# Row-tiled scores for two more head pairs, a token mixer by two pairs, and loads ordered by due time, in a block-sparse attention with a ResMLP behind it

## The chip, the cores and the metric

One core of one Trainium2 chip runs the whole program. The metric is the device time of one execution in microseconds (us). The kernel before takes 315.21 us, the median of five runs (314.22 to 315.86).

The engines are named as in the profile: PE is TensorE's matmul, PEld its weight load, DVE is VectorE, ACT is ScalarE, POOL is GpSimd and SP is SyncE. ACT, POOL and SP also issue transfers. L859 means line 859 of the kernel before.

## What is computed

Block-sparse attention over 4 batches, 8 heads, 768 positions and a head dimension of 64, and behind it a ResMLP block with a token mixer and a channel mixer. The reference, cut:

```python
scores = scale * np.matmul(q, k.transpose(0, 1, 3, 2))      # scale 1/8
mask = ...            # blocks of 32: neighbours, first and last, 3 sampled ones for each block of queries
attn = softmax(np.where(mask, scores, -1e9))
x = np.matmul(attn, v)                   # heads side by side: (4, 768, 512)
a1 = alpha1 * x + beta1
tok = np.einsum('ts,bsd->btd', w_tok, a1)                   # w_tok 768 x 768
u = x + lam * tok
a2 = alpha2 * u + beta2
out = u + lam * (np.maximum(a2 @ w_ch1, 0.0) @ w_ch2)       # w_ch1 512 x 2048, w_ch2 2048 x 512
```

All inputs and the output are 32-bit floats. The same mask serves every batch and head.

## The kernel before

**Pairs and units.** Two heads of a batch make a pair, so there are 16 pairs (`NP`), four for each batch. The scores of a pair, 9216 columns in all, are cut into 9 units of 1024 columns (`UN`), 144 units in all. Each unit goes through the scores' matmuls into a PSUM tile `sps` (there are two), one exponential on ACT (L869) into a buffer `eT` (seven), and the matmuls with the values (L895), whose stationary side is `eT` and whose moving side is `vext` with 65 columns, the last of them ones, so that the row sums come out beside the result. At the end of each head, L911 and L914 divide and write the head's columns of `x_sb`.

**Two forms of scores.** For pairs below `T0` = 6, `prep_full` turns queries and keys by PE transposes through the identity (L402, 12 for a pair) and four copies (L447 on ACT or L449 on DVE). The scores (L840) contract over 88 rows: 64 of the head and 24 that carry the mask as a bias. From pair 6 on, `prep_rows` turns them by DMA transposes that SP issues (L753 twice for the queries, L776 for the keys) into `qk`, and two more transfers from POOL (L796, called swaps below) copy query halves to the other half of the partitions. The scores (L859) then contract over 64 rows in each half of the array, the two halves beside each other, and two units are issued as one batch. The mask is not part of these scores: the exponential is multiplied by a mask tile on DVE (L876, 1024 columns). The mask tile is made once, in `mask_ops`, by 12 matmuls (L645) on the `qk` of pair `T0 - 1` and six exponentials (L666). There are two `qk` tiles, four buffers each for the loaded `q`, `k` and `v`, and three `vext`.

**The mixers.** For each pair L1061 and L1072 make `a1p`, 36 matmuls (L1107) of 128 columns multiply it by the turned token weights `wtokT` in two groups of three tiles, L1131 adds the result to `x_sb` and L1138 scales it into `ub`. `ub` is turned into `uT` by PE transposes and copies in batch 0 and for pair 15, by a DMA transpose from SP (L1203) otherwise. When the four pairs of a batch are there, the channel mixer follows in two halves: 16 times four matmuls of 384 columns (L1234), each four closed by a ReLU on ACT (L1256) or DVE (L1264) into `hts` (two buffers), then 48 matmuls of 512 columns (L1296), and L1318 and L1337 give the output out.

**Order.** The first pair is prepared by hand-written instructions before the plan: loads from SP, ACT and POOL (L352 to L363), keep-warm matmuls on zeros (L369), casts (L397), two small matmuls for the mask's rows (L407), transposes (L402), copies (L421). All the rest is ordered by `Plan`: each operation has a due time in units (about one exponential each), the engines that may run it with modelled durations, the operations that it depends on and the buffers that it needs; at each modelled instant the ready operation that is due first is emitted. `SEEDS` shifts some due times by random amounts. `pin_order` then fixes the order on each engine, so an instruction that waits on the chip holds everything behind it on its engine. The loads from memory all go over POOL's queue in one chain, `chain`, in the order of the text: pair 1, the token weights, pair 2, three vectors, pair 3, a vector and a bias, half of `w1b`, pair 4, the other half, pair 5, a quarter of `w2b`, pair 6, the rest of `w2b`, then pairs 7 to 15. Each load is modelled to land after the one before it.

Of the kernel before, what the change touches and what calls it, by code (L numbers as in the profile page):

```python
# [43 lines left out]
T0 = 6  # L44
FINE = 3
SEEDS = [4000001, 4000004, 4000014, 4000025, 4000032, 4000033, 4000038, 4000259, 4000302, 4000315, 4000516, 4000717, 4000744, 4000751, 4000754, 4000772, 4000823, 4000910, 4001214, 4001220, 4002279]
# [52 lines left out]
class Plan:  # L99
# [3 lines left out]
    def __init__(self, pools, free):  # L103
        self.pools = {k: list(range(n)) for k, n in pools.items()}
        self.free = dict(free)
        self.ops = []
        self.users = {}
        self.slot = {}
        self.held = {}
        self.reader = {}  # L110
        self.exps = 0
        self.dma = 0.0
# [47 lines left out]
    def run(self):  # L160
# [13 lines left out]
        while count:  # L174
# [4 lines left out]
            while moved:  # L179
# [35 lines left out]
                if best:  # L215
# [5 lines left out]
                    op.eng = e  # L221
                    if callable(vis):
                        vis = vis(self, t)
                    op.vis = t + vis
                    if op.reads:
                        self.reader[op.reads] = (e, op.vis)
                    self.free[e] = t + occ
# [26 lines left out]
def kernel(  # L254
# [81 lines left out]
    a1p = many(2, [P, NT, P], BF, "a1p")  # L336
    ub = many(2, [P, NT, P], BF, "ub")
# [18 lines left out]
    nc.scalar.dma_start(identb[:], ident_dr.ap())  # L356
    nc.sync.dma_start(kx2[0][MB, 0, :], ind_dr.ap())
    nc.sync.dma_start(q2f[:, 1, :], pair_ap(q, 0, 0)[:, 1, :])
    nc.sync.dma_start(k2f[:, 1, :], pair_ap(k, 0, 0)[:, 1, :])
    for i in range(1, 4):  # L360
        nc.sync.dma_start(kx2[i // 2][MB, i % 2, :], ind_dr.ap())

    nc.gpsimd.dma_start(ld["v"][0][:], pair_ap(v, 0, 0))  # L363
# [58 lines left out]
    keep_warm(5, P)  # L422
    for j in range(1, 4):
        nc.sync.dma_start(qx2[j // 2][MB, j % 2, :], qx2[0][MB, 0, :])

    nc.gpsimd.tensor_copy(out=hold[MB, :], in_=mbb[MB, :])

# [3 lines left out]
        dict(PE=5800, ACT=6100, DVE=5600, POOL=4200, SP=6500),  # L431
# [20 lines left out]
    def dma_vis(cost, issue):  # L452
        def f(plan, t):
            plan.dma = max(plan.dma, t + issue + 1200) + cost
            return plan.dma + 800 - t

        return f

    chain = [None]

    def load(name, cost, due, emit, **kw):
        op = pl.add(
            name, [("POOL", 720, dma_vis(cost, 720))], due, emit, after=chain[-1:], **kw
        )
        chain.append(op)
        return op
# [8 lines left out]
    def load_pair(pi, what="qkv"):  # L475
        b, n = divmod(pi, NPAIR)
        for w in what:
# [6 lines left out]
            LD[key] = load(("load",) + key, 1020, 9 * pi - 20, emit, need=[(key, [(w, 0)])])  # L484
# [6 lines left out]
    def bc_load(nm, t, src):  # L491
# [3 lines left out]
        BC[nm] = load(("bc", nm), 640, 0, emit)  # L495
# [24 lines left out]
    LD[("v", 0)] = landed(("v", 0), 6000)  # L520
    pl.slot[("v", 0)] = ("v", 0)
    pl.pools["v"].remove(0)
    load_pair(1)
    for g in range(3):
        WT.append(load(("wtk", g), 2500, 0, emit_wtk(g)))
    load_pair(2)
    bc_load("lam", lam_bc, moe_lam)
    bc_load("a1", a1_bc, moe_alpha1)
    bc_load("b1", b1_bc, moe_beta1)
    load_pair(3)  # L530
    bc_load("a2", a2_bc, moe_alpha2)
    BE2 = load(("be2",), 300, 0, emit_be2)
    for g in range(2):
        W1.append(load(("w1", g), 2530, 0, emit_w1(g)))
    load_pair(4)
    for g in range(2, 4):
        W1.append(load(("w1", g), 2530, 0, emit_w1(g)))
    load_pair(5)
# [24 lines left out]
    for g in range(4):  # L563
        if g == 1:
            load_pair(6)
        W2.append(
            load(("w2", g), 2530, 0, emit_w2(g), deps=[x.tr for x in WTT])
        )
    for pi in range(7, NP):
        load_pair(pi)  # L570
# [173 lines left out]
    def prep_rows(pi):  # L744
# [3 lines left out]
        def tvis(x):  # L748
            return lambda plan, t: x

        def e_q(op, h):
# [5 lines left out]
            [("SP", 900, tvis(4200))],  # L757
# [8 lines left out]
            [("SP", 900, tvis(4200))],  # L766
# [7 lines left out]
        def e_k(op):  # L774
# [8 lines left out]
            [("SP", 1300, tvis(4200))],  # L783
# [7 lines left out]
        for r in range(2):  # L791

            def e_s(op, r=r):
                i = sl(key)
                lo, hi = slice(r * D, (r + 1) * D), slice((1 - r) * D, (2 - r) * D)
                nc.gpsimd.dma_start(qx2[i][lo, :, HS:S], qx2[i][hi, :, 0:HS])  # L796
# [4 lines left out]
                    [("POOL", 720, tvis(3300))],  # L801
# [9 lines left out]
    for i in range(2):  # L811
# [5 lines left out]
            deps=[landed(("f", i), 5500 + 500 * i)],  # L817
# [571 lines left out]
```

The softmax here doesn't subtract the row's maximum and nothing guards it: scores larger than these inputs give would overflow.

## Time and profile before

| what | value |
|---|---|
| median of five runs | 315.21 us |
| time of the profiled execution | 314.9 us |
| its span, first to last instruction | 313.1 us |
| PE busy | 307.5 us |
| DVE busy | 231.4 us |
| ACT busy | 179.7 us |
| POOL busy | 55.7 us |
| scores by the full form, L840 | 144 matmuls, 33.4 us busy |
| scores by rows, L859 | 240 matmuls, 27.3 us busy |
| token mixer, L1107 | 576 matmuls, 38.2 us busy |
| mask multiplies, L876 | 90, 685 ns each |
| exponentials, L869 | 144, 1022 ns each |
| first exponential | 8.45 us |
| first L1234 of batch 0 | 57.6 us |
| last exponential | ends 244.3 us |
| first L1234 of batch 3 | 259.1 us |

How to read it: busy time of PE is modelled, and matmuls overlap, so the sum over lines is more than the time that they add. What one matmul adds is the distance from its start to the next start. The windows split the span into stretches of 10 us with the busy time of each engine in them; the chain of waits follows the work that ended last back to the start. A DMA share is the mean over 16 DMA engines, and is above 1 where several transfers share an engine.

### The profile page before, as it was taken

To read this page: it belongs to the slowest core of one execution; us is meant where nothing else is said; L and a number is where in the kernel's file an instruction comes from. 1 tells how busy PE (TensorE), PEld (TensorE's weight loads), DVE (VectorE), ACT (ScalarE), POOL (GpSimd) and SP (SyncE) were. 2 spreads that over 40 slices of the span, in tenths; PEclk is the share of its full clock that TensorE was granted. 3 is DMA by queue.
4 is the path that set the end of the run, shared out by engine and by line. 5 is a ranking of instruction groups with operands and counts; after the bars stand their busy time and mean duration, and the time that the engine had idled before them with its cause. 6 is when DMAs were issued, how large, how long until landed. Compare 5 with 4: busy or idle time off the path is not lost.

```text
span 313.1 us, 7718 instructions
## 1 busy us (share of the span) xinstructions
PE 307.5 (98%) x3252; PEld 189.1 (60%) x3252; DVE 231.4 (74%) x434; ACT 179.7 (57%) x215; POOL 55.7 (18%) x87
## 2 busy tenths in 40 slices
PE   7999999999999999999999999999999999999996
PEld 3687888765565656565656565655656555555543
DVE  4569997967797988979878686978878776565631
ACT  4899999895766686867675766557575400000000
POOL 6456443150402140304010100110000000000000
PEclk9999999999999999999999999999999999999999
DMA  8999999999356875378442322332102001100012
GB/s 180 194 236 222 209 204 206 191 118 110 75 91 111 126 115 122 98 113 128 73 110 61 78 60 61 87 75 61 27 33 61 33 2 39 62 36 33 36 51 83
DMA packets 46742, 31.40 MB, mean 100 GB/s; under 512 B 27212, under 2 KB 42292, under 8 KB 46708
## 3 DMA queue, kind: packets, MB, share of 16 engines
q0 software_dynamic: 16944, 17.44, 34.0%
q1 hardware_dynamic: 29440, 13.24, 18.0%
q8 instruction: 25, 0.41, 0.5%
q10 hardware_dynamic: 324, 0.23, 0.3%
q14 instruction: 9, 0.07, 0.1%
HBM read 30.86 MB, written 6.29 MB: 119 GB/s over the span
## 4 chain that ended last, share of the span: by engine, by line
PE 93%; DVE 3%; DMA 1%; ACT 1%; ACTq 0%; issue 0%
PE gb L1234 27%; PE gb L1296 26%; PE gb L895 12%; PE gb L1107 10%; PE sps L859 8%; PE sps L840 7%; PE gb L402 2%; DMA identb<-ident_c 1%; ACT eT L869 1%; PE sps L645 1%; DVE qk L449 1%; PE gb L600 0%; DVE x_sb L1131 0%; DVE ub L1138 0%; DVE a1p L1072 0%
## 5 line engine op out<-in xcount | busy, mean ns | idle before, releaser
L869 ACT ACTIVATE eT<-sps 128x1024 f16<-128x1024 f32 x144 | 139.9, 1022 | 36.7 <-PE sps L859 29.0
L1234 PE MATMUL gb<-uT,w1b 128*128 128x384 bf16 x512 | 100.0, 326 | 0.0
L1296 PE MATMUL gb<-w2b,hts 128*128 128x512 bf16 (+2 forms) x400 | 96.4, 370 | 0.0
L1264 DVE TENSOR_SCALAR hts<-gb,b1t 128x384 bf16<-128x384 f32 x76 | 46.9, 617 | 29.4 <-PE gb L1234 28.9
L1234 PEld LDWEIGHTS <-w1b 128*128 128x128 bf16 x512 | 46.8, 97 | 34.5 <-issue 2.0
L876 DVE TENSOR_TENSOR eT<-eT,msk 128x1024 f16<-128x1024 f16 x90 | 60.4, 685 | 6.1 <-ACT eT L869 6.1
L895 PEld LDWEIGHTS <-eT 128*128 128x128 f16 x1152 | 49.8, 98 | 21.7 <-issue 4.7
L895 PE MATMUL gb<-vext,eT 128*128 128x65 f16 x1152 | 58.1, 194 | 0.1
L1296 PEld LDWEIGHTS <-hts 128*128 128x128 bf16 x400 | 35.7, 97 | 31.2 <-issue 0.7
L1256 ACT ACTIVATE hts<-gb,b1t 128x384 bf16<-128x384 f32 x52 | 30.1, 582 | 28.1 <-PE gb L1234 26.4
L1107 PE MATMUL gb<-a1p,wtokT 128*128 128x128 bf16 x576 | 38.2, 219 | 0.1
L1107 PEld LDWEIGHTS <-wtokT 128*128 128x128 bf16 x576 | 33.9, 98 | 5.6 <-issue 2.6
L840 PE MATMUL sps<-qk 88*128 88x512 bf16 (+1 forms) x144 | 33.4, 340 | 0.3 <-ACT eT L869 0.2
L796 POOL DMA_DIRECT2D qk<-qk x20 | 12.1, 611 | 121.2 <-DMA qk<-q 58.7
L859 PE MATMUL sps<-qk 64*128 64x512 bf16 (+1 forms) x240 | 27.3, 326 | 0.0
L1318 DVE TENSOR_TENSOR ot<-x_sb,gb 128x512 f32<-128x512 f32 (+2 forms) x25 | 16.6, 664 | 10.1 <-PE gb L1296 9.6
L1131 DVE TENSOR_TENSOR x_sb<-x_sb,gb 128x384 f32<-128x384 f32 x32 | 17.7, 552 | 8.0 <-PE gb L1107 7.7
L914 DVE TENSOR_TENSOR x_sb<-gb,rcp 128x384 f32<-128x384 f32 x32 | 17.8, 558 | 1.1
L1138 DVE TENSOR_TENSOR ub<-x_sb,a_bc 128x384 bf16<-128x384 f32 x32 | 17.4, 553 | 0.5
L859 PEld LDWEIGHTS <-qk 64*128 64x128 bf16 x240 | 8.0, 94 | 15.0 <-issue 12.2
L1072 DVE TENSOR_TENSOR a1p<-a1p,b_bc 128x768 bf16<-128x768 bf16 (+1 forms) x20 | 15.8, 792 | 0.2
L1061 DVE TENSOR_TENSOR a1p<-x_sb,a_bc 128x768 bf16<-128x768 f32 (+1 forms) x20 | 15.8, 791 | 0.2
(64 smaller groups left out, 147.8 us busy)
## 6 DMA issues: line engine op xcount, KB each, us to landing
out_dram<-ot SPq DMA_DIRECT2D x23, 256.0 KB, 2.0
v<-in_v_dram POOLq DMA_DIRECT2D x16, 192.0 KB, 6.7
q<-in_q_dram POOLq DMA_DIRECT2D x15, 192.0 KB, 8.4
k<-in_k_dram POOLq DMA_DIRECT2D x15, 192.0 KB, 6.6
w1b<-in_moe_w_ch_dram POOLq DMA_DIRECT2D x4, 512.0 KB, 9.7
w2b<-in_moe_w_ch_dram POOLq DMA_DIRECT2D x4, 512.0 KB, 12.2
qk<-qk POOLq DMA_DIRECT2D x20, 96.0 KB, 2.2
wtk<-in_moe_w_tok_dram POOLq DMA_DIRECT2D x3, 384.0 KB, 8.8
```

Source lines behind the costliest of these rows:

```text
L840: nc.tensor.matmul(spsT[sl(key)][:, o : o + w], kx2[i][0:KC, a, ts(jt, P)], qx2[i][0:KC, a, c : c + w], start=True, stop=True,)
L859: nc.tensor.matmul(spsT[sl(key)][:, o : o + w], kd[i][rows, h, g, :], qx2[i][rows, h, c : c + w], start=True, stop=True,)
L869: nc.scalar.activation(eTt[sl(("eT", i))][:], spsT[sl(key)][:], AF.Exp, bias=EXPB, scale=SCALE)
L876: nc.vector.tensor_tensor(out=e, in0=e, in1=msk[:, :, x : x + 512], op=ALU.mult)
L895: nc.tensor.matmul(bk[:, t * VW : t * VW + D + 1], eTt[sl(("eT", i))][:, ts(col, P)], vx[:, a, jt, 0 : D + 1], start=(r == 0), stop=(r >= ...
L914: nc.vector.tensor_tensor(out=x_sb[:, s0 : s0 + NT, h * D : (h + 1) * D], in0=o[:, :, 0:D], in1=rc[:].unsqueeze(2).broadcast_to([P, NT, D] ...
L1107: nc.tensor.matmul(tp[:, j, :], wtokT[:, s, ts(m * g + j, P)], a1p[sl(ak)][:, s, :], start=(s == 0), stop=(s == NT - 1),)
L1131: nc.vector.tensor_tensor(out=s, in0=s, in1=tp, op=ALU.add)
L1234: nc.tensor.matmul(bank(bk)[:, 0:HS], w1b[:, dk, ts(f, P)], uT[b % 3][:, dk, ts(hf, HS)], start=(dk == 0), stop=(dk == 3),)
L1256: nc.scalar.activation(htsT[hk][:, f, :], bank(bk)[:, 0:HS], AF.Relu, bias=b1t[:, f : f + 1], scale=1.0,)
L1264: nc.vector.tensor_scalar(out=htsT[hk][:, f, :], in0=bank(bk)[:, 0:HS], scalar1=b1t[:, f : f + 1], scalar2=0.0, op0=ALU.add, op1=ALU.max,)
L1296: nc.tensor.matmul(bank(ck)[:, cs], htsT[hk][:, nk, ts(mt, P)], w2h["t"][:, nk, cs], start=(nk == 0), stop=(nk == 15),)
```

## The change

The row form of the scores starts at pair 4, the first of the second batch (`T0` = 4). The mask tile is made from pair 3's `qk`. In batches 1 to 3 the token mixer takes pairs 0 and 1, then 2 and 3 of the batch together: `a1p` and `ub` get a dimension for the pair, each L1107 matmul has 256 columns, and L1131 and L1138 run on three groups of two tiles, 512 columns, for both pairs. Pair 15's `uT` is turned by DMA as the others'. The swaps go out on SP's queue. The loads are no chain any more: each has a due time of its own, and POOL takes the one that is due first among those with a free buffer. Ahead of the plan, the identity's load and the four loads of the indicator rows stand on SP before the second head's loads, pair 0's values are issued by POOL after `hold`, and eight keep-warm matmuls stand where five stood. The plan's model of transfers, its starting times and its `SEEDS` differ (27 seeds in place of 21). The diff, cut to what the text speaks of:

```diff
-T0 = 6
+T0 = 4
...
-    a1p = many(2, [P, NT, P], BF, "a1p")
-    ub = many(2, [P, NT, P], BF, "ub")
+    a1p = many(2, [P, NT, 2, P], BF, "a1p")
+    ub = many(2, [P, 2, NT, P], BF, "ub")
...
-    nc.scalar.dma_start(identb[:], ident_dr.ap())
-    nc.sync.dma_start(kx2[0][MB, 0, :], ind_dr.ap())
+    nc.sync.dma_start(identb[:], ident_dr.ap())
+    for i in range(4):
+        nc.sync.dma_start(kx2[i // 2][MB, i % 2, :], ind_dr.ap())
     nc.sync.dma_start(q2f[:, 1, :], pair_ap(q, 0, 0)[:, 1, :])
     nc.sync.dma_start(k2f[:, 1, :], pair_ap(k, 0, 0)[:, 1, :])
-    for i in range(1, 4):
-        nc.sync.dma_start(kx2[i // 2][MB, i % 2, :], ind_dr.ap())
-
-    nc.gpsimd.dma_start(ld["v"][0][:], pair_ap(v, 0, 0))
+
...
-    keep_warm(5, P)
+    keep_warm(8, P)
     for j in range(1, 4):
         nc.sync.dma_start(qx2[j // 2][MB, j % 2, :], qx2[0][MB, 0, :])
 
     nc.gpsimd.tensor_copy(out=hold[MB, :], in_=mbb[MB, :])
+    nc.gpsimd.dma_start(ld["v"][0][:], pair_ap(v, 0, 0))
...
-        dict(PE=5800, ACT=6100, DVE=5600, POOL=4200, SP=6500),
+        dict(PE=5900, ACT=6300, DVE=5900, POOL=4700, SP=6900),
...
+    def queued(cost):
+
+
         def f(plan, t):
-            plan.dma = max(plan.dma, t + issue + 1200) + cost
-            return plan.dma + 800 - t
+            wait = max(0, plan.ring[-15] - t) if len(plan.ring) > 14 else 0
+            plan.dma = max(plan.dma, t + wait + 1900) + cost
+            plan.ring.append(plan.dma + 700)
+            plan.loads.append(plan.now)
+            plan.occ = 720 + wait
+            return plan.dma + 700 - t
 
         return f
 
-    chain = [None]
+    def beside(cost, issue):
+
+
+        def f(plan, t):
+            t0 = t + 0.6 * issue + 650
+            busy = min(cost, max(0, plan.dma - t0))
+            plan.dma += busy
+            if busy:
+                plan.ring = [x + busy if x > t0 else x for x in plan.ring]
+                for op in plan.loads:
+                    if op.vis and op.vis > t0:
+                        op.vis += busy
+                plan.shifted = True
+            return t0 + cost + busy + 750 - t
+
+        return f
 
     def load(name, cost, due, emit, **kw):
-        op = pl.add(
-            name, [("POOL", 720, dma_vis(cost, 720))], due, emit, after=chain[-1:], **kw
-        )
-        chain.append(op)
-        return op
+        return pl.add(name, [("POOL", 720, queued(cost))], due, emit, **kw)
...
-            LD[key] = load(("load",) + key, 1020, 9 * pi - 20, emit, need=[(key, [(w, 0)])])
+            LD[key] = load(
+                ("load",) + key,
+                1020,
+                9 * pi - (6 if w == "v" else 12 if pi < T0 else 20),
+                emit,
+                need=[(key, [(w, 0)])],
+            )
...
-    load_pair(1)
     for g in range(3):
-        WT.append(load(("wtk", g), 2500, 0, emit_wtk(g)))
-    load_pair(2)
-    bc_load("lam", lam_bc, moe_lam)
-    bc_load("a1", a1_bc, moe_alpha1)
-    bc_load("b1", b1_bc, moe_beta1)
-    load_pair(3)
-    bc_load("a2", a2_bc, moe_alpha2)
-    BE2 = load(("be2",), 300, 0, emit_be2)
-    for g in range(2):
-        W1.append(load(("w1", g), 2530, 0, emit_w1(g)))
-    load_pair(4)
-    for g in range(2, 4):
-        W1.append(load(("w1", g), 2530, 0, emit_w1(g)))
-    load_pair(5)
+        WT.append(load(("wtk", g), 2500, g, emit_wtk(g)))
+    bc_load("lam", lam_bc, moe_lam, 8)
+    bc_load("a1", a1_bc, moe_alpha1, 8.1)
+    bc_load("b1", b1_bc, moe_beta1, 8.2)
+    bc_load("a2", a2_bc, moe_alpha2, 16)
+    BE2 = load(("be2",), 300, 17, emit_be2)
+    for g in range(4):
+        W1.append(load(("w1", g), 2530, 24 + g, emit_w1(g)))
+    for pi in range(1, NP):
+        load_pair(pi)
...
-            load(("w2", g), 2530, 0, emit_w2(g), deps=[x.tr for x in WTT])
+            load(
+                ("w2", g),
+                2530,
+                38 + 2 * g,
+                emit_w2(g),
+                deps=[x.tr for x in WTT],
+                after=W2[-1:],
+            )
         )
-    for pi in range(7, NP):
-        load_pair(pi)
...
-            [("SP", 900, tvis(4200))],
+            [("SP", 1250, beside(480, 1250))],
...
-                nc.gpsimd.dma_start(qx2[i][lo, :, HS:S], qx2[i][hi, :, 0:HS])
+                nc.sync.dma_start(qx2[i][lo, :, HS:S], qx2[i][hi, :, 0:HS])
 
             res.append(
                 pl.add(
                     ("swap", pi, r),
-                    [("POOL", 720, tvis(3300))],
+                    [("SP", 450, beside(380, 450))],
...
+        w = n % 2 if b else 0
+        ak = ("a1p", pi - w)
+        uk = ("ub", pi - w)
         dd = base + (-3 if lastp else 4 if b == 0 else 2)
-        a2 = []
-        parts = [(0, D), (D, P)] if lastp else [(0, P)]
+        parts = [(0, D), (D, P)] if lastp and b == 0 else [(0, P)]
+        if w == 0:
+            A2 = []
...
-        uk = ("ub", pi)
+        if b and w == 0:
+            continue
         ubs = []
-        m = 3
+        wp = w + 1
+        m = 3 if w == 0 else 2
+        cs = slice(2 * (n - w) * D, (2 * n + 2) * D)
         for g in range(NT // m):
             bk = ("mmk", pi, g)
 
             tk = None
             for j in range(m):
 
-                def e_tok(op, part, g=g, j=j, bk=bk, ak=ak):
-                    tp = bank(bk)[:, 0 : m * P].rearrange("p (j c) -> p j c", j=m)
+                def e_tok(op, part, g=g, j=j, bk=bk, ak=ak, m=m, wp=wp):
                     for s in part:
                         nc.tensor.matmul(
-                            tp[:, j, :],
+                            bank(bk)[:, j * wp * P : (j + 1) * wp * P],
                             wtokT[:, s, ts(m * g + j, P)],
-                            a1p[sl(ak)][:, s, :],
+                            a1p[sl(ak)][:, s, 0:wp, :].rearrange("p w c -> p (w c)"),
...
-            def e_xu(op, g=g, bk=bk, s0=s0, cs=cs):
+            def e_xu(op, g=g, bk=bk, s0=s0, cs=cs, m=m, wp=wp):
                 s = x_sb[:, s0 + m * g : s0 + m * g + m, cs]
-                tp = bank(bk)[:, 0 : m * P].rearrange("p (j c) -> p j c", j=m)
+                tp = bank(bk)[:, 0 : m * wp * P].rearrange("p (j c) -> p j c", j=m)
                 nc.vector.tensor_tensor(out=s, in0=s, in1=tp, op=ALU.add)
 
...
-                    out=ub[sl(uk)][:, m * g : m * g + m, :],
-                    in0=x_sb[:, s0 + m * g : s0 + m * g + m, cs],
-                    in1=bc(a2_bc, m),
+                    out=ub[sl(uk)][:, 0:wp, m * g : m * g + m, :].rearrange(
+                        "p w j c -> p j w c"
+                    ),
+                    in0=x.rearrange("p j (w c) -> p j w c", w=wp),
+                    in1=a2_bc[:, cs]
+                    .rearrange("p (w c) -> p w c", w=wp)
+                    .unsqueeze(1)
+                    .broadcast_to([P, m, wp, P]),
...
-        if b == 0 or pi == NP - 1:
+        if b == 0:
...
+            for v2 in range(2):
+
+                def e_ud(op, uk=uk, b=b, n=n - 1 + v2, v2=v2):
+                    nc.sync.dma_start_transpose(
+                        uT[b % 3][:, n, :].rearrange("p (o t) -> p o t", o=NT),
+                        ub[sl(uk)][:, v2].rearrange("p o c -> p (o c)"),
+                    )
+
+                UTD[pi - 1 + v2] = [
+                    pl.add(
+                        ("utd", pi - 1 + v2),
+                        [("SP", 1250, beside(960, 1250))],
+                        dd + 3,
+                        e_ud,
+                        deps=ubs + wait,
+                        uses=[uk],
+                    )
+                ]
```

## The prediction

> **What bounds the kernel now.** I read the page's busy shares and its chain first, then the windows of ten microseconds, then the timeline of TensorE, then the transfers.
>
> The busy row and the first line of the chain of waits:
>
> ```profile
> PE 307.5 (98%) x3252; PEld 189.1 (60%) x3252; DVE 231.4 (74%) x434; ACT 179.7 (57%) x215; POOL 55.7 (18%) x87
> ```
>
> ```profile
> PE 93%; DVE 3%; DMA 1%; ACT 1%; ACTq 0%; issue 0%
> ```
>
> TensorE (PE) carries 93% of the chain. A busy PE need not be streaming, so I checked spacings: four L1296 matmuls of 512 columns stand 0.86 us apart as a group in the chain, 216 ns each, and everything in the last 50 us is of that kind. The windows say where other engines come close:
>
> ```profile
> 40.00:50.00 10.00, 10.00 (x188) 8.35 (x185) 8.84 (x18) 9.84 (x12) 5.79 (x8) 1.00 1.27 205
> 50.00:60.00 10.00, 10.00 (x169) 8.09 (x167) 8.56 (x20) 8.80 (x11) 1.43 (x2) 1.00 1.28 199
> ...
> 240.00:250.00 10.00, 10.00 (x91) 5.62 (x90) 7.89 (x15) 5.10 (x8) 0.00 (x0) 1.00 0.12 33
> ```
>
> The columns are PE, PEld, DVE, ACT and POOL busy, the clock, the DMA share and GB/s. From 10 to 60 us ScalarE (ACT, 10.00 of 10 at 20 to 30) is nearly as full as PE, VectorE (DVE) close behind, and the DMA engines are oversubscribed (share above 1). From 80 us on only PE is full. So PE work that is removed comes out of the time wholly after 80 us, and before 60 us only as far as ACT, DVE and the transfers let PE have its next work.
>
> **Scores by rows for pairs 4 and 5.** The two forms, in PE's timeline:
>
> ```profile
> 38.99 0.60 PE L840 MATMUL sps<-qk 88*128 88x256 bf16 x3
> 39.42 0.50 PE L402 MATMUL gb<-identb,ub 128*128 128x128 bf16 x6
> ...
> 87.15 0.83 PE L1107 MATMUL gb<-a1p,wtokT 128*128 128x128 bf16 x12
> 87.92 0.61 PE L859 MATMUL sps<-qk 64*128 64x256 bf16 x6
> 88.46 0.42 PE L895 MATMUL gb<-vext,eT 128*128 128x65 f16 x8
> ```
>
> A unit of the full form takes 39.42 - 38.99 = 0.43 us, so two take 0.86. A batch of two units by rows takes 88.46 - 87.92 = 0.54, and enters late: twelve L1107 matmuls at 56 ns each end at 87.82, and L859 starts 0.10 later. So 0.64. Two pairs are 18 units, 9 batches: 9 x 0.22 = 2.0 us off PE. The batch streams 1024 columns on each half of the array, 0.43 us if the halves ran side by side without loss; the other 0.21 is lost around each batch. The Trainium skill's page TensorEngine Tiling (Array Packing), section Key Properties, says that a change of tiling mode drains the engine, which speaks against this part of the change and fits that 0.21 us; its section Theoretical Speedup allows up to 2x, which would make the saving 9 x 0.43 = 3.9 us, and the row makes it 2.0.
>
> The PE transposes of these pairs go too: 2 x 12, and three take 0.17 us (12.30 to 12.48 in the timeline), 56 ns each: 1.35 us. The 12 mask matmuls (L645) only move.
>
> **Token mixer by two pairs.** 12 pairs x 36 = 432 matmuls of 128 columns at 56 ns are 24.2 us. They become 216 of 256 columns. No L1107 row has 256 columns; L840 spends 0.43 us on 1024 columns, 108 ns for 256, so 23.3 to 23.6 us: 0.7 us off, 0 to 0.9 as bounds. The weight loads halve, but they lie beside matmuls already. On DVE, 24 L1131 and 24 L1138 of 384 elements (552 ns) become 18 and 18 of 512, which I price by L1318's 664 ns: 26.5 to 23.9 us, 2.6 off an engine that isn't the bound.
>
> Pair 15's `uT` goes by DMA instead of six PE transposes: 0.35 us off PE. Its chain gets longer by 108 - 56 ns x 36 = 1.9 us of mixer, a third round of L1131/L1138 (1.3) and two SP issues of 1.2 with 3.0 to landing instead of about 1.2 of transposes and copy: 7 us or so. The cover is in this view, PE and its weight loads just before batch 3's first L1234:
>
> ```profile
> 258.24 1.03 PE L1296 MATMUL gb<-w2b,hts 128*128 128x512 bf16 x4
> 258.89 1.29 PEld L1234 LDWEIGHTS <-w1b 128*128 128x128 bf16 x8
> ```
>
> PE has batch 2's L1234 and L1296 left: about 4.3 us of each until 258.9, and another 48 L1296 of 216 ns, 10.4 us, that need no batch 3. That is 19 us against 7, so nothing; without the cover it would be 7.
>
> **ACT and DVE before 58 us.** The six mask exponentials stood at 66 to 73 us and must now precede pair 4's multiplies, about 48 us, where ACT is full; 18 multiplies are added, 8 copies fall.
>
> ```profile
> L449 DVE COPY qk<-gb 64x768 bf16<-64x768 bf16 x16 | 8.9, 555 | 4.6 <-PE gb L402 4.3
> ...
> L447 ACT COPY qk<-gb 64x768 bf16<-64x768 bf16 x6 | 4.7, 789 | 0.0
> L666 ACT ACTIVATE msk<-sps 128x768 f16<-128x768 f32 x6 | 4.7, 812 | 0.1
> ```
>
> Multiplies: 18 x 0.685 (L876's mean of 90) = 12.3 us on DVE, half of it after 58 us, where DVE has 2 to 3 us free in ten. Masks: 6 x 0.81 = 4.9 us on ACT. Copies: 8 x 0.56 to 0.79 = 4.4 to 6.3 us less, on whichever engine the plan gave them. If the copies left to DVE and ACT balance, the masks cost nothing; if all copies saved were DVE's, pair 3's last exponential (48 us), and with it the first L1234 (57.6 us), moves 4.9 us. PE would then idle for what it can't fill. I take +0.8, nearer the balance, since copies and masks are about equal; bounds 0 and +4.9.
>
> **Transposes in the full stretch.** Pairs 4 and 5 need six DMA transposes and four swaps more, at 36 to 58 us. The issues in the windows 50 to 60 and 92 to 96 us:
>
> ```profile
> qk<-q SPq DMA_TRANSPOSE x2, 7.3
> ```
>
> ```profile
> qk<-q SPq DMA_TRANSPOSE x1, 2.3
> ```
>
> In the full stretch a transpose lands after 7.3 us, later after 2.3. There are two `qk` tiles, so pair 4's second transpose waits for pair 2's last scores (about 36.5 us); it lands at 43.8, K's, issued 1.25 later, at 45. The swaps need both, and go from SP now instead of POOL: two issues of 0.45 (the cost that the plan gives them; POOL's were 0.61) and 2.2 us to landing where the queues are light, so 47; pair 4's first scores stand at 47.3 now. It just fits; if the swaps also take 7 us they are 4 late, and PE's queue is in order, so everything behind the scores waits. The same holds for pair 5. Bounds 0 and +8; I take +1.0, nearer the fitting end.
>
> Taking the swaps off POOL frees it: it sat over 120 us before them, holding loads. Loads feed nothing late now (`w1b` landed well before 57.6), so I give that nothing; the reordered loads are the same bytes in a saturated stretch, 0 either way up to the bounds above.
>
> **The start.** The first pieces of the chain:
>
> ```profile
> 1.90 4.08 DMA identb<-ident_c
> ...
> 6.02 0.80 PE gb L402 x6
> 6.81 0.53 PE gb L369 x5
> ...
> 7.38 1.89 PE sps L840 x5
> ```
>
> The identity is awaited until 5.98 us; the two L407 before it are done near 5.35. Earlier it gains at most 0.65. Three more keep-warm matmuls cost 3 x 0.11 = 0.3 if nothing hides them. `v` of pair 0 is issued 2.9 us later, behind L426: it landed at 5.5, its copy L933 started at 7.7, and its first use is 10.55, so landing by 10.1 costs nothing. The second head's loads stand behind four small issues more (0.4 each): landing near 7.8 and 8.3 instead of 6.2 and 6.7, casts at 7.2 and 7.5 slip by 0.8, hidden under the first four units' exponentials. Matmuls here take twice their later time (six L402 in 0.80 us, 0.34 later), though the clock row reads full; if the denser start ended that sooner, up to 1.5 us more (half of the 3 us of matmuls between 9 and 12.3). I take -0.3; bounds -2.0 and +1.0. The skill's page TensorE: Matmul & The Clock Gate, section Part 1, has the clock at half until some 3.4 us of sustained activity have passed in a free-running window; by it the filled gap before 7.4 could bring full rate forward by a whole window, and the start would be near -1.8 instead of the -0.3 that the rows carry.
>
> **The sum.** PE work: -2.0 - 1.35 - 0.7 - 0.35 = -4.4. Start -0.3, masks +0.8, transposes +1.0: -2.9. The profiled execution took 314.9 us (span 313.1, 1.8 around it), 0.3 below the median of the five: 312.0 there, 312.3 as a median.
>
> **Rivals.**
> (a) *Late transposes decide.* For: 7.3 us, and a DMA share of 1.3 from 44 to 64 us. Against: pair 4's first head can start earlier, and the loads may be spread more. With the swaps 4 us late at both pairs: -4.4 - 0.3 + 0.8 + 8 = +4.1, 319.3; it turns into a loss from 2 us late at each pair. Chance 0.16.
> (b) *ACT takes the bound up to the first L1234.* The masks' 4.9 us stand whole: -4.4 - 0.3 + 4.9 + 0.5 = +0.7, 315.9; half of it paid gives 313.5. For: ACT 9.84 of 10. Against: the 8 copies that fall. Chance 0.14.
> (c) *The start gives more.* Full rate 1.5 to 2 us sooner and transposes in time: -4.4 - 1.8 + 0.5 = 309.5. For: only L840 and L402 at double time up to 12 us. Against: the first exponentials wait on copies, not on rate alone. Chance 0.12.
> (d) *The end is exposed*, if 7 us of the last chain show: 319. The 19 us of cover speak against it: 0.02.
>
> **How the numbers follow.** The forecast, 312.3 with its own range 310.3 to 314.2, has 0.56. About 0.3% is what can be told from no change: 314.3 to 316.2. Faster: forecast 0.56, (c) 0.12, a little of (b) 0.02: 0.70. Same: most of (b) 0.09 and the mild end of (a) 0.03: 0.12. Slower: 0.18 from (a), the rest of (b) and (d). The range reaches to (c) below and to (b)'s full price above: 309.3 to 316.2.
>
> **What would show it.** L840's count falls from 144 to 96, L859's rises from 240 to 288, the mixer has 144 narrow and 216 wide matmuls near 109 ns apart. Right: PE without gaps from 13 us on, first L1234 within 2 us of 57.6. Wrong by (a): score matmuls of pair 4 or 5 waiting on a DMA of `qk`, around 47 and 57 us; by (b): first L1234 past 61 us with PE idle on ACT; by (c): 56 ns transposes before 10 us. The forecast falls if PE idles over 5 us between 15 and 80 us.

## The result

| | before | after |
|---|---|---|
| median | 315.3 us (45 runs) | 318.6 us (24 runs) |
| time over before, with its 95% interval | 1 | 1.0086 (1.0070 to 1.0102) |
| profiled execution, span | 314.9, 313.1 us | 316.9, 315.1 us |
| mean granted clock in it, as a share of full speed | 0.999 | 0.989 |
| first exponential | 8.45 us | 8.12 us |
| first matmul of the channel mixer, batch 0 | 57.6 us | 62.2 us |

The changed kernel is slower by 0.9%, outside the forecast's range (309.3 to 316.2) and near rival (a)'s 319.3. The ratio leaves disturbed executions out; the medians hold all. Helper lines moved: L840 is now L867, L859 is L886, L1107 is L1138, L1234 is L1280, L869 is L896, L402 is L410, L753 and L776 are L780 and L803, L796 is L823.

The page of after, its busy row, the shares of the chain, the clock in 40 slices, and the groups of the two forms of scores and of the mixer:

```profile
PE 306.2 (97%) x3009; PEld 184.0 (58%) x3009; DVE 226.7 (72%) x411; ACT 184.8 (59%) x228; POOL 43.2 (14%) x67
...
PEclk9999999699999999999999999999999999999999
...
PE 87%; DMA 8%; ACT 2%; SPq 1%; issue 1%; DVE 1%; ACTq 0%
...
L1138 PE MATMUL gb<-a1p,wtokT 128*128 128x256 bf16 (+1 forms) x360 | 36.9, 259 | 0.0
L886 PE MATMUL sps<-qk 64*128 64x512 bf16 (+1 forms) x288 | 34.0, 332 | 2.2 <-DMA qk<-qk 2.2
...
L867 PE MATMUL sps<-qk 88*128 88x512 bf16 (+1 forms) x96 | 22.6, 341 | 1.5 <-DMA qk<-qk 1.0
```

The counts are those forecast (96, 288, 360). New are the last columns: PE idles 2.2 us before row scores and 1.0 before full ones, each time for a transfer `qk<-qk`. The chain holds 8% DMA where it held 1%, and one slice of the clock reads 6. The windows of after, columns as in the prediction:

```profile
40.00:50.00 10.00, 9.50 (x143) 6.86 (x140) 6.20 (x13) 9.59 (x12) 3.26 (x6) 1.00 1.36 163
50.00:60.00 10.00, 7.82 (x121) 5.93 (x118) 5.93 (x16) 5.05 (x6) 3.37 (x5) 0.73 1.24 202
60.00:70.00 10.00, 10.00 (x111) 6.31 (x108) 8.90 (x17) 8.73 (x12) 2.14 (x3) 0.93 1.32 185
```

From 50 to 60 PE was full before; now it is busy for 7.82 of 10 at a clock of 0.73. After 80 us the stretches are as full as before. To size it, I summed over PE's matmuls the distance to the next start less the columns divided by 2.4, less 2.5 ns. That is the pace of the full clock in these traces: 56 ns for 128 columns, 216 for 512. The one-column matmuls count 25 ns, the spacing at which they run here, and row scores half where two run side by side. What is left, idle time, half clock and changes of tiling together, is 28.0 us against 20.3, and the streaming itself 287.2 against 292.8: +7.7 - 5.6 = +2.1, the spans' difference of 2.0. By stretch, the losses grew at 20 to 30 us (0.7 to 1.6), 40 to 50 (0.1 to 1.4) and above all 50 to 60 (0.1 to 5.2). Up to 20 us they did not grow (6.6 before, 6.5 after).

The chain of waits of after at that place (start, duration, what), and PE's timeline there:

```profile
38.48 8.89 DMA qk<-q
47.45 0.72 SPq L823
48.22 7.07 DMA qk<-qk
55.33 1.01 PE sps L886 x4
```

```profile
52.28 0.49 PE L410 MATMUL gb<-identb,ub 128*128 128x128 bf16 x6
53.44 0.37 PE L886 MATMUL sps<-qk 64*128 64x512 bf16 x1 [0.66 <-DMA qk<-qk]
55.33 1.01 PE L886 MATMUL sps<-qk 64*128 64x512 bf16 x5 [1.52 <-DMA qk<-qk]
56.27 0.59 PE L630 MATMUL gb<-be2b,w1b 128*128 128x1 bf16 x16
56.72 2.72 PE L1138 MATMUL gb<-a1p,wtokT 128*128 128x128 bf16 x24
```

Pair 4's second query transpose takes 8.9 us, the swap behind it 7.1, and pair 4's first scores, which stood at 47.3 before, start at 53.4 and 55.3. PE's starts leave gaps of 0.8 and 1.7 us. Then 24 mixer matmuls take 59.23 - 56.72 = 2.5 us where 24 x 56 ns are 1.35: the clock is at half. The same in two windows of 5 us, and the microsecond in which the clock fell:

```profile
50.00:55.00 5.00, 3.15 (x68) 2.29 (x66) 3.94 (x11) 3.11 (x4) 1.95 (x3) 0.96 1.23 213
55.00:60.00 5.00, 4.67 (x53) 3.63 (x52) 1.98 (x5) 1.94 (x2) 1.43 (x2) 0.50 1.25 192
```

```profile
54.00:55.00 1.00, 0.00 (x0) 0.00 (x0) 0.05 (x1) 0.00 (x0) 0.46 (x1) 0.78 1.25 204
```

So 2.5 us of gaps and some 2.3 us of half clock, the rest of 5.1 being changes of tiling. A mean of 0.78 from 54 to 55 puts the fall at about 54.6 us, inside the second gap: PE had then been idle for 0.8 us and, after one score matmul, for another 0.9. The Trainium skill's page TensorE: Matmul & The Clock Gate, section Part 1, has the clock fall to half after an idle window of about 3.4 us. Here 1.7 us of idle time in two pieces came before the fall, so in this trace less was enough.

A smaller stall is at the start. The chain of after:

```profile
6.15 6.60 DMA qk<-qk
12.88 0.38 PE sps L867
```

The copies of the mask's rows (L432, from SP at 6.15) land at 12.75, and the second head of pair 0 stands at 11.5: 1.0 us of waiting. They follow the four indicator loads on SP's queue, and `k`, `v` and the token weights are in flight beside them.

### The profile page after: what moved, and what is told of

Read it like the earlier page. It is cut to its first block, busy times and chain, and to the rows that moved or that the text cites. A ratio compares the mean times of both kernels' runs of the same rounds, so it can differ in the third digit from the quotient of the medians.

```text
span 315.1 us, 7202 instructions
## 1 busy us (share of the span) xinstructions
PE 306.2 (97%) x3009; PEld 184.0 (58%) x3009; DVE 226.7 (72%) x411; ACT 184.8 (59%) x228; POOL 43.2 (14%) x67
## 4 chain that ended last, share of the span: by engine, by line
PE 87%; DMA 8%; ACT 2%; SPq 1%; issue 1%; DVE 1%; ACTq 0%
PE gb L1280 27%; PE gb L1342 26%; PE gb L922 11%; PE gb L1138 10%; PE sps L886 10%; DMA qk<-qk 4%; DMA qk<-q 3%; ACT eT L896 2%; PE sps L867 2%; PE gb L410 1%; DMA qk<-ind_c 1%; DVE qk L458 0%; ACT wtokT L456 0%; SPq L823 0%; PE gb L630 0%
## 5 line engine op out<-in xcount | busy, mean ns | idle before, releaser
L896 ACT ACTIVATE eT<-sps 128x1024 f16<-128x1024 f32 x144 | 139.7, 1024 | 43.5 <-PE sps L886 40.2
L1280 PE MATMUL gb<-uT,w1b 128*128 128x384 bf16 x512 | 98.4, 326 | 0.0
L903 DVE TENSOR_TENSOR eT<-eT,msk 128x1024 f16<-128x1024 f16 x108 | 72.5, 685 | 10.9 <-ACT eT L896 10.8
L1280 PEld LDWEIGHTS <-w1b 128*128 128x128 bf16 x512 | 46.7, 97 | 34.1 <-issue 2.8
L1310 DVE TENSOR_SCALAR hts<-gb,b1t 128x384 bf16<-128x384 f32 x61 | 37.6, 616 | 25.8 <-PE gb L1280 25.3
L1302 ACT ACTIVATE hts<-gb,b1t 128x384 bf16<-128x384 f32 x67 | 38.4, 584 | 24.8 <-PE gb L1280 23.8
L1138 PE MATMUL gb<-a1p,wtokT 128*128 128x256 bf16 (+1 forms) x360 | 36.9, 259 | 0.0
L886 PE MATMUL sps<-qk 64*128 64x512 bf16 (+1 forms) x288 | 34.0, 332 | 2.2 <-DMA qk<-qk 2.2
L1138 PEld LDWEIGHTS <-wtokT 128*128 128x128 bf16 x360 | 30.5, 102 | 6.2 <-issue 2.3
L867 PE MATMUL sps<-qk 88*128 88x512 bf16 (+1 forms) x96 | 22.6, 341 | 1.5 <-DMA qk<-qk 1.0
L1162 DVE TENSOR_TENSOR x_sb<-x_sb,gb 128x512 f32<-128x512 f32 (+1 forms) x26 | 16.7, 643 | 8.2 <-PE gb L1138 8.1
L886 PEld LDWEIGHTS <-qk 64*128 64x128 bf16 x288 | 9.9, 94 | 18.9 <-issue 15.6
L508 POOL DMA_DIRECT2D v<-in_v_dram x15 | 10.7, 711 | 47.8 <-DVE vext L960 36.8
L1176 DVE TENSOR_TENSOR ub<-x_sb,a_bc 128x512 bf16<-128x512 f32 (+1 forms) x26 | 16.5, 646 | 0.3
L508 POOL DMA_DIRECT2D q<-in_q_dram x15 | 10.7, 712 | 39.4 <-DMA qk<-k 23.5
```

Source lines behind the costliest of these rows:

```text
L508: nc.gpsimd.dma_start(ld[w][sl(key)][:], pair_ap(src, b, n))
L867: nc.tensor.matmul(spsT[sl(key)][:, o : o + w], kx2[i][0:KC, a, ts(jt, P)], qx2[i][0:KC, a, c : c + w], start=True, stop=True,)
L886: nc.tensor.matmul(spsT[sl(key)][:, o : o + w], kd[i][rows, h, g, :], qx2[i][rows, h, c : c + w], start=True, stop=True,)
L896: nc.scalar.activation(eTt[sl(("eT", i))][:], spsT[sl(key)][:], AF.Exp, bias=EXPB, scale=SCALE)
L903: nc.vector.tensor_tensor(out=e, in0=e, in1=msk[:, :, x : x + 512], op=ALU.mult)
L1138: nc.tensor.matmul(bank(bk)[:, j * wp * P : (j + 1) * wp * P], wtokT[:, s, ts(m * g + j, P)], a1p[sl(ak)][:, s, 0:wp, :].rearrange("p w c ...
```

## The experiments

The times are medians, the ratios against before on the same chip.

**e1_keys_moving.** Pairs 4 and 5 stream turned keys in place of turned queries, so no swap and no query transpose stands ahead of their scores.

```diff
-                    qx2[i][rows, h, c : c + w],
+                    (kx2 if pi < 6 else qx2)[i][rows, 0 if pi < 6 else h, c : c + w],
```

> The changed kernel, with the same order of instructions on every engine, but the scores of pairs 4 and 5 stream the turned keys in place of the turned queries, so they no longer wait for the query transposes and the swaps (all transfers are still issued; the scores of these two pairs are not the reference's). Theory (the swaps are late): PE's waits on swaps at 52 to 55 us, 2.5 us, go, the granted clock stays full between 55 and 63 us, the first L1280 comes 3 to 6 us earlier than 62 us, and the median falls by 4 to 6 us from 318.6 to 313 to 315; what is left late is the keys' transpose. Rival (ACT or the new order holds PE up there): the wait only changes its name, and the time stays above 317.

314.9 us (12 runs), 1.0002 (0.9980 to 1.0024); first L1280 at 58.3. The waits of PE and the 5-us windows:

```profile
PE sps L867 <- DMA qk<-qk: 2.3, 1, 2.3
PE sps L886 <- DMA qk<-k: 1.4, 1, 1.4
```

```profile
50.00:55.00 5.00, 4.70 (x108) 3.68 (x107) 4.75 (x13) 4.50 (x6) 2.05 (x3) 1.00 1.24 211
55.00:60.00 5.00, 5.00 (x74) 3.93 (x73) 4.48 (x9) 4.05 (x6) 1.50 (x3) 1.00 1.25 195
```

3.7 us of the median come back with one edit (4 to 6 were expected), 0.0084 of the time (2.6 us) by the ratios. The hole and the half clock at 50 to 60 are gone; a wait for the key transpose stays, and the one at the start is 2.3 in this execution.

**e5_no_swap_wait.** The same pairs stream only query columns that no swap writes.

```diff
-                    qx2[i][rows, h, c : c + w],
+                    (
+                        qx2[i][rows, :, 0 : w // 2]
+                        if pi < 6
+                        else qx2[i][rows, h, c : c + w]
+                    ),
```

> The changed kernel in the same order, but the scores of pairs 4 and 5 stream the first columns of both heads' turned queries, which the query transposes write and the swaps don't (same count and width of matmuls; the scores of these two pairs are not the reference's). The swaps are still issued. If the swaps are the late step, this is as fast as the kernel that streams keys, 314 to 316, and PE waits on a transpose for 1 us at most near 52 us. If the transposes themselves come too late, PE still waits over 2 us there and the time is 316.5 or more.

315.4 us (10 runs), 1.0007 (0.9987 to 1.0026), as e1: its only wait on `qk` from 15 us on is for the keys' transpose, 1.5 us. So of the two steps in a row the swap is the one that is waited for; the transpose alone nearly fits.

**e2_start_old.** The changed kernel with the start of before: identity from ACT, one indicator load ahead, `v` first on POOL, five keep-warm matmuls, the old times in the plan.

```diff
-    nc.sync.dma_start(identb[:], ident_dr.ap())
-    for i in range(4):
-        nc.sync.dma_start(kx2[i // 2][MB, i % 2, :], ind_dr.ap())
+    nc.scalar.dma_start(identb[:], ident_dr.ap())
+    nc.sync.dma_start(kx2[0][MB, 0, :], ind_dr.ap())
...
+    nc.gpsimd.dma_start(ld["v"][0][:], pair_ap(v, 0, 0))
...
-    keep_warm(8, P)
+    keep_warm(5, P)
```

> The changed kernel with the start of the kernel before: identity behind the keys on ACT's queue, three of the four indicator loads behind the second head's loads, pair 0's values first on POOL, five keep-warm matmuls. Theory (swaps decide): the first scores of the second head, which wait 1.2 us for the mask rows at 11.5 us, come in time, the first exponential moves 0.3 us later, and the stall at 52 us stays: 317 to 319. Rival (the start is what was lost): the time falls to 315 or less.

316.1 us (12 runs), 1.0034 (1.0018 to 1.0049), between the two expectations. The waits of PE (L887 is L886 of after):

```profile
PE sps L887 <- DMA qk<-qk: 2.7, 2, 2.2
PE gb L379 <- DVE warm L375: 1.2, 1, 1.2
PE sps L417 <- DMA qk<-ind_c: 0.8, 1, 0.8
PE gb L412 <- DMA identb<-ident_c: 0.7, 1, 0.7
```

The wait of the second head for the mask's rows is gone, the one for the swap stays. The new start, with the order that its times give, costs the changed kernel about 0.0052 x 315 = 1.6 us (the medians differ by 2.5); the two profiled executions, 1.0 us apart, show less, and up to 20 us PE lost 6.3 us here against 6.5 in after. Where the 1.6 us arise isn't shown.

**e7_keys_start_old.** e1 and e2 together.

> Both in one: pairs 4 and 5 stream keys (no wait for queries and swaps), and the start of the kernel before. Theory (two stalls of the same kind, small SP transfers behind a full DMA stretch, are what keeps the forecast from coming true): the gains add, 312 to 313.7, near the forecast of 312.3. Rival (a third loss, in ACT or the order): 314.5 or more.

313.2 us (4 runs), 0.9941 (0.9921 to 0.9962). The two gains add. With neither stall, most of what the change removes is there: within 0.9 us of the forecast by the median, and by the ratio 1.9 us off the time before, where 2.9 was forecast.

**e3_mixer_only.** The kernel before with the mixer by two pairs and pair 15's `uT` by DMA, nothing else.

```diff
-    a1p = many(2, [P, NT, P], BF, "a1p")
-    ub = many(2, [P, NT, P], BF, "ub")
+    a1p = many(2, [P, NT, 2, P], BF, "a1p")
+    ub = many(2, [P, 2, NT, P], BF, "ub")
...
-                            a1p[sl(ak)][:, s, :],
+                            a1p[sl(ak)][:, s, 0:wp, :].rearrange("p w c -> p (w c)"),
...
-        if b == 0 or pi == NP - 1:
+        if b == 0:
```

> The kernel before with the token mixer by two pairs alone. Theory: PE loses 0.7 us of mixer and 0.35 us of transposes, DVE loses some operations, the end stays covered: 0.7 to 1.3 us faster than before, 314.0 to 314.6. Rival (the longer chain of the last pairs shows at the end): slower than before by up to 3 us, with PE idle after 250 us.

313.7 us (12 runs), 0.9963 (0.9950 to 0.9977): 1.2 us off, where the terms say 0.7 + 0.35. DVE is at 225.6 us of 231.4, and the end isn't exposed.

**e6_fill_gap.** Twelve matmuls of zeros, 512 columns each (2.6 us), ahead of pair 4's first scores: the swap is as late, but PE streams meanwhile.

```diff
+            if batch[0] == 36:
+                for _ in range(12):
+                    nc.tensor.matmul(
+                        spsT[sl(keys[0])][:, 0:512], warm[:, 0:P], warm[:], start=True, stop=True
+                    )
```

> The changed kernel with 12 matmuls of zeros (512 columns, 216 ns each, 2.6 us) ahead of pair 4's first scores, into the score tile that these overwrite. They fill the gap in which PE waits for the swaps and add nothing while the wait is longer than they are. If the drop of the granted clock after the gap costs as much as the gap, the clock stays near full between 55 and 63 us and the median falls by 1.5 to 3.5 us against 318.6, to 315 to 317. If the gap alone costs the time, nothing is gained: 318 to 320.

317.2 us (6 runs), 1.0071 (1.0048 to 1.0094), just short of the gain expected. The 5-us windows:

```profile
50.00:55.00 5.00, 5.00 (x111) 4.10 (x110) 4.23 (x12) 4.52 (x5) 1.55 (x3) 1.00 1.25 201
55.00:60.00 5.00, 4.70 (x51) 2.54 (x50) 1.71 (x6) 2.10 (x3) 1.86 (x3) 1.00 1.22 207
```

The clock stays full, and the stretch from 50 to 60 loses 1.1 us beside the zeros' 2.6, against after's 5.2 in all. In the medians it is 1.4 us, and the intervals of the two ratios overlap: the mechanism is shown by the clock row, its price in time only roughly. Its profiled execution lost 2.3 us more than after's at 10 to 20 us. There its matmuls ran at half rate until about 17.4 us, those of after until 10.2: three L867 take 1.06 us at 14.41, where three take 0.60 at 13.52 in after.

**e8_w2_held.** In the plan, `w2b`'s loads depend on pair 4's preparation, to empty the DMA stretch.

```diff
+    for op in W2:
+        op.deps.append(PREP[4][-1])
```

> The changed kernel with the four loads of w2b held back until pair 4's keys are turned, by the plan's order on POOL; PE's planned order up to 70 us is the same. Four loads of 2.6 us each leave the DMA stretch from 44 to 66 us. If the full DMA stretch is why the swaps land 7 us after their issue, they land earlier here (3 to 6 us), PE's wait near 52 us shrinks below 1.5 us, and the time falls to 314.5 to 317. If the transposes and swaps are slow by themselves, nothing changes: 317.5 to 319.5.

319.9 us (4 runs), 1.0165 (1.0136 to 1.0194). It didn't do what it was made for, as this window shows (DMA share in the last column but one):

```profile
40.00:45.00 5.00, 4.50 (x43) 2.58 (x39) 2.49 (x4) 4.11 (x5) 2.14 (x3) 0.76 1.59 123
```

POOL issued other loads in the same place; the share rose from 1.37 to 1.59, and pair 4's swap could go out only 12.2 us after the issue of its second query transpose, where after has 9.0. It tells nothing of an emptier queue, and supports no theory.

**e9_loads_gated.** So the loads were held on the chip: POOL first copies from what pair 4's swap wrote, ahead of `w2b` and of every load from pair 6 on.

```diff
+    gate = pl.add(
+        ("gate",),
+        [("POOL", 400, 500)],
+        -100,
+        lambda op: nc.gpsimd.tensor_copy(
+            out=hold[:], in_=qx2[sl(("qk", 4))][:, 0, HS : HS + NBLK]
+        ),
+        deps=PREP[4],
+        uses=[("qk", 4)],
+    )
+    for op in W2 + [LD[(x, pi)] for pi in range(6, NP) for x in "qkv"]:
+        op.deps.append(gate)
```

> The changed kernel with one small copy on POOL that reads what pair 4's swaps write, ahead of all loads of pairs 6 and later and of w2b; the order on PE is the same to the last instruction. On the chip POOL now stands there until the swaps have landed, so the load queue runs empty near 47 to 49 us. If the full DMA stretch is what makes small transfers slow, the swaps land 2 to 4 us after their issue in place of 7.1, PE's wait of 2.5 us near 52 us goes, and the first L1280 comes at 57 to 59 us. Later loads come later, so the time may be lost again after 60 us: 314 to 318. If transposes and swaps are slow by themselves, the swaps still take 6 us or more and the wait stays.

321.4 us (4 runs), 1.0220 (1.0191 to 1.0249), above the 314 to 318 expected. The swap's issues in after, and then in this run (count, size, median us to landing), and this run's windows:

```profile
qk<-qk SPq DMA_DIRECT2D x2, 96.0 KB, 7.1
```

```profile
qk<-qk SPq DMA_DIRECT2D x2, 96.0 KB, 2.2
```

```profile
45.00:50.00 5.00, 5.00 (x78) 3.79 (x77) 2.04 (x6) 4.63 (x6) 0.00 (x0) 1.00 0.70 64
50.00:55.00 5.00, 4.66 (x108) 3.64 (x106) 4.82 (x13) 4.50 (x6) 4.57 (x7) 1.00 0.62 87
...
60.00:65.00 5.00, 3.08 (x32) 1.68 (x30) 1.60 (x3) 3.62 (x6) 1.43 (x2) 1.00 1.32 166
65.00:70.00 5.00, 2.82 (x19) 1.38 (x20) 4.14 (x8) 1.78 (x2) 1.20 (x2) 0.67 1.23 211
```

The same two transfers of 96 KB land in 2.2 us with the DMA share at 0.70 and in 7.1 with it at 1.23 to 1.34. PE no longer waits for them, and the first L1280 starts at 58.3. The time is worse all the same, because the held loads are late further on:

```profile
53.79 12.01 DMA w2b<-in_moe_w_ch_dram
65.80 0.02 issue
65.82 0.69 DVE w2b L656
```

This is the chain of the same run: DVE's cast of `w2b` waits until 65.8 us, the mask multiply behind it in DVE's queue waits with it, and PE loses 4.1 us. This execution took 318.6 us; what the others lost beyond it isn't shown. The loads can't simply be moved; their bytes are wanted soon after.

The gate does what the swaps themselves did in the kernel before. There POOL issued them and stood idle ahead of them for 121.2 us in all, so the loads behind them waited, and its 20 swaps landed in 2.1 to 3.4 us; the 24 from SP in after took 2.3 to 7.1. No run issues pair 4's swaps from POOL in the changed kernel, so what their move to SP costs by itself isn't shown.

**e10_t0_4_late_model and e4_t0_5_late.** The change kept, but its plan is told that transposes and swaps are late while loads fill the queues. e4 also moves the row form to pair 5 on; e10 keeps pair 4. New seeds were picked in both by the plan's own modelled end, and a pair's first query transpose now follows the preparation of the pair before it in the plan, so latency, seeds and this order changed together.

```diff
-            return t0 + cost + busy + 750 - t
+            late = (5500 if issue > 1000 else 4500) if plan.dma > t0 + 3000 else 0
+            return t0 + cost + busy + 750 + late - t
...
             deps=[LD[("q", pi)]],
+            after=PREP[pi - 1][-1:],
```

> The changed kernel with the row form from pair 5 on, and a plan that models transposes and swaps in a full DMA stretch as 5.5 and 4.5 us later, with seeds searched for that model. Theory: pair 5's transfers have pair 4's nine units and the first channel mixer to hide behind, so PE doesn't wait on a transfer of qk, the clock stays full, and 1.0 us (one pair's rows) + 0.7 (transposes) + 1.05 (mixer) come out: 312 to 313.5. Rival (something else in the changed order costs the time): 315 or more.

> The changed kernel with pairs 4 and 5 still by rows, and a plan that models transposes and swaps in a full stretch as 5.5 and 4.5 us later, seeds searched for it. If the loss is a plan that trusts its transfers too early, the plan now has other work for PE while pair 4 is late, and the time comes to 313 to 315. If the wait can't be planned away because pair 4's transposes can't begin before pair 2's scores are done, 316 or more.

e4: 313.1 us (6 runs), 0.9943 (0.9921 to 0.9964). e10: 312.5 us (4 runs), 0.9927 (0.9906 to 0.9948), the best here, faster than both kernels. In e10 the swaps are as late as in after, and PE doesn't wait for them (issues, then PE's timeline):

```profile
qk<-qk SPq DMA_DIRECT2D x2, 96.0 KB, 7.8
```

```profile
51.18 0.94 PE L631 MATMUL gb<-be2b,w1b 128*128 128x1 bf16 x32
53.08 1.67 PE L1140 MATMUL gb<-a1p,wtokT 128*128 128x128 bf16 x27 [0.95 <-DVE a1p L1102]
54.67 0.61 PE L888 MATMUL sps<-qk 64*128 64x512 bf16 x6
...
55.90 1.66 PE L1282 MATMUL gb<-uT,w1b 128*128 128x384 bf16 x8
```

Pair 4's scores stand at 54.67, behind 27 mixer matmuls; the channel mixer starts at 55.9 where it was 57.6 before and 62.2 after. The wait that is left is 0.95 us for `a1p`, and the clock is full in all its windows from 40 to 70 us.

**e11_t0_5_late_start_old.** e4 with the old start and new seeds.

> The kernel with rows from pair 5 on and the corrected model, which took 313.1, with the start of the kernel before and seeds searched again. The wait of the second head's mask rows near 11.5 us goes, 0.3 us of the earlier first exponential is given back: 312 to 313. If the start doesn't matter there, 313 to 313.5.

313.7 us (12 runs), 0.9956 (0.9933 to 0.9979): a miss, no gain over e4. PE hardly waits, but its clock halves, as its timeline shows:

```profile
50.04 0.55 PE L632 MATMUL gb<-be2b,w1b 128*128 128x1 bf16 x16
50.45 0.59 PE L870 MATMUL sps<-qk 88*128 88x512 bf16 x3
50.88 0.54 PE L632 MATMUL gb<-be2b,w1b 128*128 128x1 bf16 x16
51.29 1.01 PE L870 MATMUL sps<-qk 88*128 88x512 bf16 x2
```

From 51.3 on the full scores take twice their time, with no idle time ahead of them.

**e12_pe_rows.** The row form from pair 4, but pairs 4 and 5 turned by PE transposes and eight copies each, with the old start and new seeds.

```diff
-            PREP[pi] = prep_rows(pi)
+            PREP[pi] = (prep_rows_pe if pi < 6 else prep_rows)(pi)
```

> Scores by rows from pair 4 on, but pairs 4 and 5 turned by PE transposes and eight copies each from PSUM (queries to both halves of the partitions) in place of DMA transposes and swaps; corrected model, start of the kernel before, seeds searched. PE gives up 1.35 us of transposes, keeps the 2.0 us of rows and 1.05 of mixer, and no scores wait on a transfer before pair 6: 312 to 313.5. If the copies (16 of some 0.36 us) or the masks hold ACT and DVE up before 58 us, 314 or more.

313.4 us (12 runs), 0.9960 (0.9940 to 0.9979). No late transfer, first L1280 at 58.3; the PE transposes are paid again.

## Why the prediction was wrong

**The step that failed** is the term for the transposes in the full stretch: "It just fits; if the swaps also take 7 us they are 4 late", taken at +1.0. The transposes were priced by a row of the full stretch (7.3 us; measured 8.9), the swaps by rows where the queues are light (2.2; measured 7.1), though both run in the same stretch. With 7 us for the swaps the prediction's own chain ends near 52; the transposes went out 2.0 us later than it had them (38.5 for 36.5) and took 1.6 more, which makes the 55.3 of the chain. e5 shows that the swap is the late step, and e9 why: at a DMA share of 0.70 it is 2.2 us again. I also gave nothing for taking the swaps off POOL, though its standing still before them had held the loads back; no run prices that by itself. The Trainium skill's page DMA: Bandwidth & Descriptors, section Queues, rings and completion order, has each DMA engine take turns between queues by packets. That a small transfer lands three times later beside full load queues agrees with it.

**Half the loss had no term.** I priced the wait, not what follows it. The gaps are 2.5 us at one pair, not 4 at two: the plan had put pair 4's scores later than before, and pair 5's came in time. The other half is the clock, which e6 keeps full by filling the gap. So rival (a) had the right mechanism and place, and its time from other pieces: one late pair and a slow clock for two late pairs. That its 319.3 comes so near is luck in part. Its chance of 0.16 was too low, since the one row at hand for a transfer in that stretch spoke for it.

**The start**, -0.3, has the wrong sign by e2. The first exponential came 0.3 us earlier, as forecast, but the copies of the mask's rows land at 12.75 us. I counted what the move delays for the second head's loads, and nothing for these copies. PE's wait for them was 1.0, 2.3, 1.9, 0.7, 0.5 and 2.2 us in the profiles of after, e1, e5, e6, e8 and e9, and e2 puts the whole at about +1.6. Why they are late stays open: SP issues them at 6.15 us in after and 6.21 in e2, behind the four indicator loads in both, and in e2 PE didn't wait for them. The start also varies: up to 20 us PE lost 5.3 to 8.8 us in those six profiles, and 6.3 to 6.6 in before, e2 and e7. By the spacing of the matmuls the full rate came sooner in all six but e6's (17.4 us): at 5.0 to 10.2 us, where it came for good at 11.1 to 12.3 in the other three. That is rival (c)'s mechanism, but in after it gained nothing, since the second head's first scores start at 12.9 us as they did before.

**Right:** PE's work. -4.4 was forecast; streaming fell by 5.6, and nine more batches by rows give back about 0.2 each (the prediction's 0.21 lost around a batch), 1.8, which is -3.8. e3 gives -1.2 for the mixer and pair 15 where the terms say -1.05. With the stalls away the time is 313.2 (e7) and 312.5 (e10), against 312.3; by the ratios they are 1.9 and 2.3 us off the time before, against 2.9. **The masks** (+0.8): PE waits 0.5 us for an exponential ahead of a mask matmul at 43.2; rival (b) didn't come. That the first L1280 is past 61 us isn't its sign here, since PE waits on a transfer. **The end** is covered: nothing is lost on PE after 250 us. Rival (c)'s gain didn't come.

The forecast was to fall "if PE idles over 5 us between 15 and 80 us". PE waited some 3 us there (2.2 for `qk`, 0.5 at the masks, the rest for exponentials), and the forecast fell nevertheless: the mark left out the half clock.

What stays open: how e10's gain splits between the latency in its plan, its seeds and its order, what the 0.9 us more at 20 to 30 us are, and how much of after's wider spread is the start and how much the clock. Over the runs that the ratio uses, the time follows the granted clock of the run: 315.0 at 0.995 (one run), 317.8 at 0.989 (mean of 13), 318.9 at 0.983 to 0.984 (mean of 7).

## What to carry to other kernels

Price a transfer by a row from the stretch in which it will run, every step of a chain of transfers for itself, and let a hand-made plan know it: late data costs an in-order PE nothing where the plan puts other work first (e10). A gap on PE is to be priced with the half clock that may follow it, about as long again here. When issues at a start are moved, price every transfer that PE waits for there, the small copies too.

## What was not expected of the hardware

- The clock fell to half when PE had been idle for 1.7 us in two pieces. In after, PE had 32 matmuls of one column, six transposes and two mask matmuls just before; in e11 the clock fell at 51.3 us with no gap at all, after 48 one-column matmuls, transposes and mask matmuls of 24 rows since 47.6. That matmuls which fill little of the array count as little work is a reading of these two rows; it wasn't tried by itself.
- A 96 KB transfer from SP took 2.2 us at a DMA share of 0.70 and 7.1 to 7.8 at 1.2 to 1.3; a transpose 8.9 us in after, where the prediction's row had 7.3.
- Order in the plan is no wait on the chip: e8 moved `w2b` and got more traffic in the stretch, since the engine's next loads came up sooner.
